# Retention and gated MLP on one core: the first chunk in 128-token blocks, weight flushing by a mask from ScalarE, and a new plan

## The chip, the core and the metric

The kernel runs on one core of one Trainium2 chip. The metric is the device time of one execution in microseconds; before the change it is 221.97 us, the median of three runs (221.79 to 222.39). All inputs start in HBM and the output ends there.

## What is computed

A retention layer (8 heads, 4 sequences of 768 tokens, head size 64) is followed by a gated MLP on the 512 joined columns:

```python
for t in range(S):
    state = gamma[None, :, None, None] * state + np.einsum('bhd,bhe->bhde', k[:, :, t], v[:, :, t])
    y[:, :, t] = scale * np.einsum('bhd,bhde->bhe', q[:, :, t], state)
x = y.transpose(0, 2, 1, 3).reshape(B, S, H * D)
for k in range(K):                       # K = 5, causal taps
    gate_pre += conv_w[k][None, None, :] * xp[:, k:k + S, :]
gate = 1.0 / (1.0 + np.exp(-gate_pre))
val = x @ w_val
return gate * val @ w_out
```

The weights come as 8-byte words and are turned into float32 on the chip; values below a threshold become zero.

## The kernel before, in words

The 768 tokens are cut into 6 chunks of 128, so there are 24 attention blocks (4 sequences per chunk), numbered chunk by chunk. Block `g` has one tile `att` of 1 MB (q and k by head column, v and k by token). POOL scales v by a decay (`decay`, L253). A block is worked as two 64-token halves in 64x64 pieces of the array: `scores` (L262), the triangle `mask` (L271, VectorE), `y_scores` and `y_state` (both recorded at L299), and `state` (L283), which adds to the running state `z_ps` in PSUM. `y_state` reads a copy of that state, `snap` (L294, ScalarE), one per half; in the first chunk the first half has none. `evac` (L344, VectorE) multiplies the result in PSUM by a decay table and writes it to the chunk's `x`. Function `block` issues on TensorE, in this order, `y_scores(g)`, the second `state` of `g`, the first `state` of `g+1`, `y_state(g)`, and `scores(g+1)`.

When the four blocks of a chunk are done, `x` of 512 tokens is ready. ScalarE rounds it to `xh` (L353), POOL makes the remainder `xl` (L357). `val` (L468) is 12 matmuls of 128x512 for each of 4 column groups: wvh by xh, wvl by xh, wvh by xl. The gate is a convolution of 5 taps: tap 0 on ScalarE (L443), the others on VectorE (L445), of which the planner may move taps 1 and 2 to TensorE (`pe_tap`, L454, by a diagonal matrix). Then come the sigmoid (L461), `gated` (L477), a split into gvh (L484) and gvl (L488), and `outp` (L496), 12 matmuls for each of 4 sequences. So 48 tiles of 12 matmuls follow one another over the program.

`convert` makes one of 8 weight tiles (and the small `cw`) in seven steps: VectorE `cv_bits` (L388), `cv_top` (L394), `cv_exp` (L400), `cv_rest` (L404), ScalarE `cv_size` (L409), POOL `cv_sum` (L413), VectorE `cv_flush` (L417). Then ScalarE rounds (L428) and POOL takes the remainder (`cv_low`, L432). Its working tile `acc` comes from a ring of two PSUM banks, which the convolution uses too.

The order on every engine is fixed when the program is built. Each step is entered with a due time, an engine, a cost and what it reads and writes (`at`); `plan` (L57) is a list scheduler that runs these costs forward and writes the steps out in the order in which it started them. Each engine then works through its own queue in that order, and an instruction that waits holds all that stand behind it. SP's queue issues the loads and stores, ScalarE's queue the four small loads. The constants that steer it are `EARLY`, `EARLY_AT`, `LATE_AT`, `MLP_AT`, `W_AT` and the like (from L532).

Of the kernel before, what the change touches and what calls it, by code (L numbers as in the profile page):

```python
# [16 lines left out]
P = 128  # L17
# [39 lines left out]
def plan(steps):  # L57
# [46 lines left out]
    for s in steps:  # L104
        clock.setdefault(s.engine, 0.0)
        if not s.waits:
            offer(s)
    order, words, paged, small = [], PAGE - 32, [0.0, 0.0], False
    while any(free.values()):
# [15 lines left out]
        clock[e] = start + s.cost  # L125
        if e == "PE" and s.words:

            left, now = s.words, start
            while left >= words:
                now += s.cost * words / s.words  # L130
# [5 lines left out]
            clock[e] = max(clock[e], now + s.cost * left / s.words)  # L136
# [17 lines left out]
def tile_retention_gated_mlp(  # L154
# [52 lines left out]

    small_sb = const.tile([P, small.shape[1]], F32, name="small_sb")
    vd_sb = small_sb[:, 0:48].rearrange("p (c x) -> p c x", x=8)
    ra_sb = small_sb[:, 48:72].rearrange("p (c x) -> p c x", x=4)  # L210
    tri_sb = small_sb[:, 72:136]
    pos_sb = const.tile([2, P + 512], F32, name="pos_sb")
# [20 lines left out]

    tiles, us, snaps, xs, xh, xl, decs, pos_ps = {}, {}, {}, {}, {}, {}, {0: base}, []
# [43 lines left out]
    def state(g, s):  # L278
        b, c = chunks[g]
        v, k = halves(g, 2), halves(g, 3)  # L280
        for j in range(2):
            for x, rows, cols in ((0, LO, LO), (1, LO, HI), (0, HI, HI), (1, HI, LO)):
# [4 lines left out]
                    start=g == 0 and s == 0 and j == 0, stop=True,  # L287
                    skip_group_check=True,
                )

    def snap(g, s):
        b, c = chunks[g]
        sn = mlp.tile([P, 2, 2, HALF], F32, name="snap", bufs=4)
        nc.scalar.copy(sn, z_ps[:, :, b])  # L294
        snaps[g, s] = sn

# [15 lines left out]
    def y_state(g):  # L312
        b, c = chunks[g]
        q = halves(g, 0)
        for s in (1, 0):
            if c == 0 and s == 0:
                continue
# [61 lines left out]
    def cv_bits(n):  # L379
        hi, _ = words(n)  # L380
        size = hi.shape[1]
        bits = ps_a.tile([P, 512], I32, name="acc")[:, 0:size]
        cvt[n] = (
            bits,
# [3 lines left out]
        nc.vector.tensor_scalar(  # L388
            bits, hi, 3, 0x3FFFFFFF, op0=ALU.logical_shift_left, op1=ALU.bitwise_and
# [8 lines left out]
    def cv_exp(n):  # L398
        bits, top, _ = cvt[n]
        nc.vector.tensor_scalar(bits, top, -0x800000, None, op0=ALU.bitwise_and)  # L400

    def cv_rest(n):
        bits, _, rest = cvt[n]
# [4 lines left out]
    def cv_size(n):  # L408
        nc.scalar.activation(cvt[n][0].bitcast(F32), words(n)[0].bitcast(F32), AF.Abs)  # L409

    def cv_sum(n):
        _, top, rest = cvt[n]
        nc.gpsimd.tensor_tensor(rest, rest, top.bitcast(F32), op=ALU.add)  # L413

    def cv_flush(n):
        bits, _, rest = cvt[n]
        nc.vector.scalar_tensor_tensor(  # L417
            cw_sb.rearrange("p a k -> p (a k)") if n == "cw" else rest,
            bits.bitcast(F32), TINY, rest, op0=ALU.is_ge, op1=ALU.mult,
# [112 lines left out]

    MM = 0.232
    EARLY = 6
    EARLY_AT = 8.0
    EARLY_STEP = 4.0
    LATE_AT = 29.71
    LATE_STEP = 6.095
    MLP_AT = 30.972
    MLP_STEP = 3.476  # L540
    SPLIT_LEAD = 5.44
    CONV_LEAD = 6.919
    W_AT = (9.3, 13.0, 15.63, 22.7, 36.8, 30.28, 34.86, 38.1)
# [3 lines left out]
    def load_at(due, g):  # L547
        loaded[g] = due
        a = [("att", g % LB, "qk"), ("att", g % LB, "vk")]
        if g == 0:  # L550
# [7 lines left out]
            for s in steps[-4:]:  # L558
                s.lag = 5.0
# [24 lines left out]

    def attention(g, t, before):
# [19 lines left out]
        pairs = 64 + 16 * (c < NCH - 1) + 48 * (g + 1 < NG) - 16 * (c == 0)  # L605
# [3 lines left out]
        if b == 0:  # L609
            xbufs[c] = Slot("x", XB)  # L610
            last = [xbufs[c - 1]] + [("x", c - 1, i) for i in range(B)] if c else []
# [213 lines left out]
```

## Time and profile before

| | |
|---|---|
| median of three runs | 221.97 us |
| the profiled execution's own time | 222.85 us |
| its span in the profile | 221.1 us |
| TensorE (PE) busy | 203.8 us, 92% |
| VectorE (DVE) busy | 136.4 us, 62% |
| ScalarE (ACT) busy | 104.6 us, 47% |
| GpSimd (POOL) busy | 105.6 us, 48% |
| moved by DMA | 36.32 MB |

The profile is of one execution. "Busy" is the time in which an engine had an instruction in work; times are from the span's start. The chain of waits follows the last instruction back to what released it, step by step, so its pieces add up to the span.

### The profile page before, as it was taken

The numbers are of one execution on the slowest core, as the hardware profiler recorded it, in microseconds if no ns is written. First come the engines' busy times: TensorE is split into PE (matmuls) and PEld (weight loads), VectorE is DVE, ScalarE is ACT, GpSimd is POOL, SyncE is SP. The second block draws the span as 40 slices with busy tenths as digits, with TensorE's granted clock in tenths as the row PEclk, the third lists the DMA queues.
The fourth block names the chain that finished last, engine by engine and source line by source line (L and its number), as shares of the span: only waits on it lengthen the run. The fifth ranks groups of instructions, "written<-read, shape, count | busy, mean of one in ns | idle before, by whom it ended". The sixth has DMA issues, their size and how long they took to land.

```text
span 221.1 us, 7950 instructions
## 1 busy us (share of the span) xinstructions
PE 203.8 (92%) x3553; PEld 162.8 (74%) x3553; DVE 136.4 (62%) x211; ACT 104.6 (47%) x218; POOL 105.6 (48%) x93
## 2 busy tenths in 40 slices
PE   8467369999799999999999999999999999999994
PEld 3266358887577888788887888788878888888883
DVE  0486577999998999478386376873397543911000
ACT  2472257562965566463383464534535336331311
POOL 0274868686999726644460934600924226220400
PEclk9857557999999999999999999999999999999999
DMA  6999998653364643564456444011011111111122
GB/s 196 417 421 417 409 396 341 256 193 101 138 203 184 238 129 160 193 204 159 136 224 235 167 119 205 1 52 47 7 50 47 47 47 50 47 47 47 47 98 95
DMA packets 8822, 36.32 MB, mean 164 GB/s; under 512 B 1106, under 2 KB 1618, under 8 KB 5844
## 3 DMA queue, kind: packets, MB, share of 16 engines
q1 hardware_dynamic: 8352, 35.66, 42.5%
q8 instruction: 28, 0.46, 0.9%
q10 hardware_dynamic: 436, 0.16, 0.3%
q14 instruction: 6, 0.05, 0.1%
HBM read 29.52 MB, written 6.29 MB: 162 GB/s over the span
## 4 chain that ended last, share of the span: by engine, by line
PE 82%; DVE 6%; DMA 5%; issue 3%; POOL 3%; SPq 0%; ACT 0%; POOLq 0%; ACTq 0%
PE mm L496 30%; PE mm L468 29%; PE sy L299 12%; PE z_ps L283 5%; PE sy L262 5%; DMA att<-in_att_dram 5%; DVE u L271 2%; POOL att L253 1%; DVE top L394 1%; DVE x L344 1%; PE acc L454 1%; POOL rest L413 1%; DVE acc L388 1%; POOL wol L432 1%; DVE gate L477 1%
## 5 line engine op out<-in xcount | busy, mean ns | idle before, releaser
L445 DVE SCALAR_TENSOR_TENSOR acc<-x,cw_sb,acc 128x512 f32<-128x512 f32 x93 | 67.9, 751 | 13.9 <-ACT acc L443 12.7
L357 POOL TENSOR_TENSOR xl<-x,xh 128x512 fp32r<-128x512 f32 x24 | 30.4, 1288 | 34.9 <-PE mm L468 22.4
L488 POOL TENSOR_TENSOR gvl<-gate,gvh 128x512 fp32r<-128x512 f32 x24 | 30.7, 1289 | 29.3 <-ACT gvh L484 19.6
L496 PE MATMUL mm<-wol,gvh 128*128 128x512 f32 (+1 forms) x100 | 39.2, 392 | 0.1
L253 POOL TENSOR_TENSOR att<-att,small_sb 128x512 f32<-128x512 f32 x24 | 25.0, 1043 | 29.9 <-DMA att<-in_att_dram 24.4
L496 PE MATMUL mm<-woh,gvh 128*128 128x512 f32 (+1 forms) x100 | 39.2, 392 | 0.0
L496 PE MATMUL mm<-woh,gvl 128*128 128x512 f32 (+1 forms) x100 | 38.6, 386 | 0.0
L468 PE MATMUL mm<-xh,wvh 128*128 128x512 f32 x96 | 28.1, 406 | 1.0 <-DVE gate L477 1.0
L477 DVE TENSOR_TENSOR gate<-mm,gate 128x512 f32<-128x512 f32 x24 | 16.5, 687 | 19.4 <-PE mm L468 18.9
L299 PEld LDWEIGHTS sy<-u,att 64*64 64x64 f32 x768 | 14.9, 148 | 17.8 <-DVE u L271 11.6
L506 ACT COPY o_sb<-mm 128x512 f32<-128x512 f32 (+1 forms) x25 | 14.3, 573 | 28.5 <-PE mm L496 28.4
L468 PE MATMUL mm<-xl,wvh 128*128 128x512 f32 x96 | 27.2, 399 | 0.1
L484 ACT CAST gvh<-gate 128x512 fp32r<-128x512 f32 x24 | 14.9, 621 | 26.0 <-DVE gate L477 18.7
L299 PE MATMUL sy<-u,att 64*64 64x64 f32 x768 | 18.4, 240 | 9.3 <-DVE u L271 9.3
L468 PE MATMUL mm<-xh,wvl 128*128 128x512 f32 x96 | 26.5, 396 | 0.0
L344 DVE TENSOR_TENSOR x<-sy,dec 128x512 f32<-128x512 f32 x20 | 13.7, 686 | 19.9 <-PE sy L262 19.7
L461 ACT ACTIVATE gate<-acc 128x512 f32<-128x512 f32 x24 | 14.3, 597 | 18.4 <-POOL gvl L488 13.2
L496 PEld LDWEIGHTS mm<-wol,gvh 128*128 128x128 f32 x100 | 18.8, 188 | 4.8 <-POOL wol L432 0.9
L468 PEld LDWEIGHTS mm<-xh,wvh 128*128 128x128 f32 x96 | 17.6, 188 | 5.9 <-ACT xh L353 1.8
L496 PEld LDWEIGHTS mm<-woh,gvh 128*128 128x128 f32 x100 | 18.8, 188 | 4.3
L496 PEld LDWEIGHTS mm<-woh,gvl 128*128 128x128 f32 x100 | 18.8, 188 | 4.0
L468 PEld LDWEIGHTS mm<-xl,wvh 128*128 128x128 f32 x96 | 17.8, 187 | 4.7 <-POOL xl L357 0.4
(46 smaller groups left out, 264.9 us busy)
## 6 DMA issues: line engine op xcount, KB each, us to landing
att<-in_att_dram SPq DMA_DIRECT2D x23, 1024.0 KB, 5.8
out_dram<-o_sb SPq DMA_DIRECT2D x23, 256.0 KB, 2.0
wst<-in_w_dram SPq DMA_DIRECT2D x8, 512.0 KB, 8.7
att<-in_att_dram SPq DMA_DIRECT2D x2, 512.0 KB, 5.1
out_dram<-o_sb SPq DMA_DIRECT2D x2, 128.0 KB, 1.7
small_sb<-in_small_dram ACTq DMA_DIRECT2D x1, 68.0 KB, 4.8
eye_sb<-in_eye_dram ACTq DMA_DIRECT2D x1, 64.0 KB, 8.9
cw_raw<-in_conv_w_dram ACTq DMA_DIRECT2D x1, 20.0 KB, 6.6
```

Source lines behind the costliest of these rows:

```text
L253: nc.gpsimd.tensor_tensor(v, v, vd_sb[:, c, :].unsqueeze(2).broadcast_to([P, 8, HALF]), op=ALU.mult)
L299: return nc.tensor.matmul(sy[cols, h, off:off + HALF], lhsT=lhsT, rhs=rhs, start=start, stop=True, skip_group_check=True,)
L344: nc.vector.tensor_tensor(xs[c][:, :, b, HALO:].rearrange("p (h j) t -> p h j t", h=2), sy[:, :, 256:512].rearrange("p h (j t) -> p h j t" ...
L357: nc.gpsimd.tensor_tensor(xl[n, ct], xs[n][:, ct, :, HALO:], xh[n, ct].bitcast(F32), op=ALU.subtract)
L445: nc.vector.scalar_tensor_tensor(acc, x[:, :, k:k + P], cw_sb[:, m, k:k + 1], acc, op0=ALU.mult, op1=ALU.add,)
L461: nc.scalar.activation(gate[n, m], accs.pop((n, m)), AF.Sigmoid)
L468: nc.tensor.matmul(vps[n, m], lhsT=w[:, m, ct * P:(ct + 1) * P], rhs=xx[n, ct].rearrange("p b t -> p (b t)"), start=(i == 0), stop=(i == 3 ...
L477: nc.vector.tensor_tensor(gv, vps.pop((n, m)), gv, op=ALU.mult)
L484: nc.scalar.copy(gvs[n, m][0], gate[n, m])
L488: nc.gpsimd.tensor_tensor(gvl, gate.pop((n, m)), gvh.bitcast(F32), op=ALU.subtract)
L496: nc.tensor.matmul(ops[n, b, cs.start][:, 0:cs.stop - cs.start], lhsT=gg[:, b * P:(b + 1) * P], rhs=w[:, ct, cs], start=(i == 0), stop=(i ...
L506: nc.scalar.copy(o_sb[:, 0:step], ops.pop((n, b, cs.start))[:, 0:step])
```

## The change

1. The four blocks of chunk 0 (no earlier state) are no longer cut into halves. `wide_scores` makes the 128x128 scores of each head with 64 contraction rows (two row halves of the array); two `wide_mask` steps on VectorE apply a 128x128 triangle; `wide_y` multiplies by v over all 128 tokens, with the result in a bank of the `mm` ring in the layout of `x`; `wide_state` adds all 128 tokens to the state. There is no `snap` in these blocks. `wide_evac` reads the `mm` bank. The host lays v, k and the decay of chunk 0 out by whole tokens, and `small` grows by the triangle, from 136 to 264 columns.
2. `convert`: ScalarE makes a mask in three passes (`cv_size`, `cv_sign`, `cv_keep`) ahead of `cv_bits`, which now ands with it; `cv_exp` writes to SBUF in place of PSUM; `cv_sum` writes the result, and `cv_flush` is gone.
3. The planner knows a slow TensorE clock, the start constants are new, the first weight tile is loaded ahead of the first attention tile, and ScalarE's table load stands ahead of the four small loads.

```diff
+    def wide_scores(g):
+        q, kT = tiles[g][:, 0], tiles[g][:, 1]
+        for x in range(2):
+            for j in range(2):
+                for r, rows in enumerate((LO, HI)):
+                    nc.tensor.matmul(
+                        sy[:, r, (2 * x + j) * P:(2 * x + j + 1) * P],
+                        lhsT=kT[rows, x, j, :], rhs=q[rows, x, j, :],
+                        start=True, stop=True, skip_group_check=True,
+                    )
+    def wide_mask(g, r):
+        us[g, r] = mlp.tile([P, UT], F32R, name="gvl", bufs=GV)...
+        nc.vector.tensor_tensor(us[g, r], sy[:, r]..., wide_sb..., op=ALU.mult)
+    def wide_y(g):
+        ys[g] = ps_m.tile([P, NPAIR, P], F32, name="mm")
+        for ct in range(NPAIR):
+            for i, cols in enumerate((LO, HI)):
+                x, r, j = place(2 * ct + i)
+                nc.tensor.matmul(
+                    ys[g][cols, ct], lhsT=v[:, 2 * ct + i], rhs=u[r][:, 2 * x + j],
+                    start=True, stop=True, skip_group_check=True,
+                )
+    def wide_state(g):
...
+                nc.tensor.matmul(
+                    z_ps[(LO, HI)[r], x, b, j], lhsT=k[:, 2 * ct + i], rhs=v[:, 2 * ct + i],
+                    start=g == 0 and j == 0, stop=True, skip_group_check=True,
+                )
+    def wide_evac(g):
+        nc.vector.tensor_tensor(xs[0][:, :, g, HALO:], ys.pop(g), base, op=ALU.mult)
...
+        nc.scalar.activation(cvt[n][0].bitcast(F32), hi.bitcast(F32), AF.Abs)
+    def cv_sign(n):
+        nc.scalar.activation(m, m, AF.Sign, bias=tiny[:, 0:1])
+    def cv_keep(n):
+        nc.scalar.activation(m, m, AF.Relu, scale=KEEP)
     def cv_bits(n):
-        nc.vector.tensor_scalar(
-            bits, hi, 3, 0x3FFFFFFF, op0=ALU.logical_shift_left, op1=ALU.bitwise_and
+        nc.vector.scalar_tensor_tensor(
+            bits, words(n)[0], 3, bits, op0=ALU.logical_shift_left, op1=ALU.bitwise_and
         )
     def cv_exp(n):
-        nc.vector.tensor_scalar(bits, top, -0x800000, None, op0=ALU.bitwise_and)
+        nc.vector.tensor_scalar(rest.bitcast(I32), top, -0x800000, None, op0=ALU.bitwise_and)
     def cv_rest(n):
-            rest, words(n)[1], 2.0 ** -36, bits.bitcast(F32), op0=ALU.mult, op1=ALU.mult
+            rest, words(n)[1], 2.0 ** -36, rest, op0=ALU.mult, op1=ALU.mult
-    def cv_flush(n):
-            bits.bitcast(F32), TINY, rest, op0=ALU.is_ge, op1=ALU.mult,
...
-    EARLY = 6
-    EARLY_AT = 8.0
-    EARLY_STEP = 4.0
-    LATE_AT = 29.71
-    W_AT = (9.3, 13.0, 15.63, 22.7, 36.8, 30.28, 34.86, 38.1)
+    FIRST_LOADS = ((1, 0), (0, 0), (0, 1), (0, 2), (1, 1), (0, 3), (1, 2), (1, 3), (0, 4))
+    EARLY = 8
+    WIDE_AT = 5.173
+    WIDE_STEP = 2.417
+    LATE_AT = 15.786
+    W_AT = (7.61, 15.38, 16.24, 22.7, 36.8, 30.28, 34.04, 43.78)
```

What the plan makes of it, at three places. TensorE, the blocks of chunk 0: before, one such block (`sy` the scores and the result, `u` the masked scores, `z_ps` the state):

```order
L299 MATMUL sy<-u,att 64x64 x16
L283 MATMUL z_ps<-att 64x64 x16
L299 MATMUL sy<-att,snap 64x64 x8
L262 MATMUL sy<-att 64x64 x16
L299 MATMUL sy<-u,att 64x64 x16
```

TensorE at the same place now, from the last two blocks of chunk 0 (L328 scores, L353 result, L364 state) over block 4 to the first matmuls of the MLP (L549):

```order
L328 MATMUL sy<-att 128x128 x8
L353 MATMUL mm<-gvl,att 64x128 x8
L364 MATMUL z_ps<-att 64x64 x8
L305 MATMUL z_ps<-att 64x64 x8
L284 MATMUL sy<-att 64x64 x16
L535 MATMUL acc<-x,diag 128x512
L378 MATMUL sy<-u,att 64x64 x16
L305 MATMUL z_ps<-att 64x64 x16
L378 MATMUL sy<-att,snap 64x64 x16
L284 MATMUL sy<-att 64x64 x16
L549 MATMUL mm<-xh,wvh 128x512 x4
```

The next block's scores stand behind this block's state, as before behind `y_state`; block 4 still stands ahead of the first MLP matmul, and a tap by the diagonal matrix (L535) has come in front of block 4.

ScalarE around the end of chunk 0, before (L409 `cv_size`, L428 the rounded weight, L294 `snap`, L443 tap 0, L353 the rounded `x`):

```order
L428 CAST wvh<-rest 128x512
L294 COPY snap<-z_ps 128x256
L409 ACTIVATE acc<-wst 128x512
L294 COPY snap<-z_ps 128x256
L443 ACTIVATE acc<-x,cw_sb 128x512
L339 COPY x<-x 128x16x4
L332 ACTIVATE dec<-base,small_sb 128x128
L353 CAST xh<-x 128x512 x3
L428 CAST wvh<-rest 128x512
```

ScalarE there now (L464, L468, L472 the three mask passes, L509 the rounded weight, L430 the rounded `x`):

```order
L464 ACTIVATE acc<-wst 128x512
L468 ACTIVATE acc<-acc,tiny 128x512
L315 COPY snap<-z_ps 128x256
L472 ACTIVATE acc<-acc 128x512
L416 COPY x<-x 128x16x4
L524 ACTIVATE acc<-x,cw_sb 128x512
L315 COPY snap<-z_ps 128x256 x2
L509 CAST wvh<-rest 128x512
L430 CAST xh<-x 128x512 x4
L524 ACTIVATE acc<-x,cw_sb 128x512
```

The casts of `x` now stand behind two snapshots of the state in block 4 and a weight, where before they stood behind tap 0.

POOL from the third weight on, now (L275 decay, L498 `cv_sum`, L513 the weight's remainder, L434 the remainder of `x`); before, two `xl` stood ahead of the fourth `wvl`, and the other two a decay behind it:

```order
L498 TENSOR_TENSOR rest<-rest,top 128x512
L275 TENSOR_TENSOR att<-att,small_sb 128x512
L513 TENSOR_TENSOR wvl<-rest,wvh 128x512
L434 TENSOR_TENSOR xl<-x,xh 128x512
L498 TENSOR_TENSOR rest<-rest,top 128x512
L275 TENSOR_TENSOR att<-att,small_sb 128x512
L513 TENSOR_TENSOR wvl<-rest,wvh 128x512
L434 TENSOR_TENSOR xl<-x,xh 128x512 x3
```

Between the first and the second `xl` there are now three other steps. TensorE has 2 taps by the diagonal matrix in place of 3, VectorE 94 in place of 93.

## Rows read from the trace of the kernel before

**Rows 1.** The page: busy time by engine, clock in 40 slices, one load.

```profile
PE 203.8 (92%) x3553; PEld 162.8 (74%) x3553; DVE 136.4 (62%) x211; ACT 104.6 (47%) x218; POOL 105.6 (48%) x93
...
PEclk9857557999999999999999999999999999999999
...
small_sb<-in_small_dram ACTq DMA_DIRECT2D x1, 68.0 KB, 4.8
```

**Rows 2.** Chain of waits, chunk 0 to first MLP matmuls: start, length, what.

```profile
1.17 5.64 DMA att<-in_att_dram
...
16.05 1.14 PE sy L299 x32
...
18.89 0.75 PE sy L262 x31
...
21.01 0.69 PE sy L299 x32
...
22.18 1.91 issue
...
31.60 0.69 DVE x L344
...
32.94 1.13 PE sy L299 x32
34.07 0.85 PE z_ps L283 x32
...
36.57 1.59 PE mm L468 x6
38.15 0.86 PE acc L454 x2
```

**Rows 3.** Chain of waits, later: a tile and a block at the full clock.

```profile
80.63 2.52 PE mm L468 x10
83.16 2.80 PE mm L496 x12
85.96 0.62 PE sy L299 x32
86.58 0.47 PE z_ps L283 x32
```

**Rows 4.** Windows: busy time of each engine, then the granted clock.

```profile
36.50:66.00 29.50, 27.61 (x711) 21.36 (x705) 28.70 (x47) 18.10 (x41) 24.12 (x22) 1.00 0.52 185
66.00:72.50 6.50, 6.44 (x144) 4.76 (x145) 5.59 (x10) 3.83 (x9) 6.50 (x6) 1.00 0.48 171
```

**Rows 5.** Windows of half a microsecond in which the granted clock changed.

```profile
19.00:19.50 0.50, 0.50 (x28) 0.46 (x23) 0.00 (x0) 0.00 (x0) 0.46 (x1) 0.70 0.97 401
22.50:23.00 0.50, 0.00 (x0) 0.00 (x0) 0.47 (x2) 0.00 (x0) 0.50 (x1) 0.71 0.94 393
36.00:36.50 0.50, 0.50 (x25) 0.43 (x20) 0.00 (x0) 0.50 (x3) 0.50 (x1) 0.64 0.76 287
```

**Rows 6.** Timeline, POOL and ScalarE: start, length, engine, line, what.

```profile
10.91 1.04 POOL L253 TENSOR_TENSOR att<-att,small_sb 128x512 f32<-128x512 f32 x1 [2.91 <-DMA att<-in_att_dram]
19.04 1.04 POOL L253 TENSOR_TENSOR att<-att,small_sb 128x512 f32<-128x512 f32 x1 [0.30 <-DMA att<-in_att_dram]
33.39 1.64 ACT L353 CAST xh<-x 128x512 fp32r<-128x512 f32 x3
34.07 2.52 POOL L357 TENSOR_TENSOR xl<-x,xh 128x512 fp32r<-128x512 f32 x2 [1.32 <-ACT xh L353]
```

**Rows 7.** Groups on VectorE up to 72 us: busy us, mean ns.

```profile
L400 DVE TENSOR_SCALAR acc<-top 128x512 int32<-128x512 int32 x8 | 5.5, 687 | 0.1
L417 DVE SCALAR_TENSOR_TENSOR rest<-acc,rest 128x512 f32<-128x512 f32 x8 | 5.5, 684 | 0.2 <-POOL rest L413 0.2
```

**Rows 8.** The same view on ScalarE up to 72 us.

```profile
L294 ACT COPY snap<-z_ps 128x256 f32<-128x256 f32 x20 | 6.8, 373 | 3.7 <-PE z_ps L283 3.5
L409 ACT ACTIVATE acc<-wst 128x512 f32<-128x512 f32 x8 | 5.2, 646 | 3.4 <-DVE rest L404 3.3
```

More of the change, by code (lines that the diff above doesn't have):

```diff
@@ L104, in plan @@
     for s in steps:
-        clock.setdefault(s.engine, 0.0)
+        clock.setdefault(s.engine, 2.2 if s.engine == "DMA" else 0.0)
         if not s.waits:
@@ L108, in plan, with dim, light @@
     order, words, paged, small = [], PAGE - 32, [0.0, 0.0], False
+    lit = {}
+    def dim(t):
+        w = int((t - FIRST) // GRID)
+        return w > 0 and lit.get(w - 1, 0.0) < 0.7 * GRID
+    def light(a, b):
+        while a < b:
+            w = int((a - FIRST) // GRID)
+            end = min(b, FIRST + (w + 1) * GRID)
+            lit[w] = lit.get(w, 0.0) + end - a
+            a = end + 1e-9
     while any(free.values()):
@@ L124, in plan @@
             small = s.small
-        clock[e] = start + s.cost
+        cost = s.cost * (DIM if e == "PE" and s.words and dim(start) else 1.0)
+        clock[e] = start + cost
         if e == "PE" and s.words:
@@ L135, in plan @@
             words -= left
-            clock[e] = max(clock[e], now + s.cost * left / s.words)
+            clock[e] = max(clock[e], now + cost * left / s.words)
+        if e == "PE":
+            light(start, clock[e])
         for t in s.next:
@@ L286, in state @@
                     rhs=v[rows, x, j, s, :],
-                    start=g == 0 and s == 0 and j == 0, stop=True,
-                    skip_group_check=True,
+                    start=False, stop=True, skip_group_check=True,
                 )
@@ L377, in words, with cv_size @@
         return raw[:, :, 1], lo16
-    def cv_bits(n):
+    def cv_size(n):
         hi, _ = words(n)
         size = hi.shape[1]
-        bits = ps_a.tile([P, 512], I32, name="acc")[:, 0:size]
         cvt[n] = (
-            bits,
+            ps_a.tile([P, 512], I32, name="acc")[:, 0:size],
             stage.tile([P, size], I32, name="top"),
@@ L563, in first_block @@
     def first_block():
-        scores(0)
-        state(0, 0)
+        state(B, 0)
+        scores(B)
     def block(g):
@@ L583, in tile_retention_gated_mlp, with first_attention @@
     scored, whole = {}, {}
+    def first_attention(g, t):
+        qk, vk = ("att", g % LB, "qk"), ("att", g % LB, "vk")
+        sc, u, y = Slot("s", 1), [Slot("gvl", GV), Slot("gvl", GV)], Slot("mm", 2)
+        at(t, "POOL", 1.0, ["small"], [vk], decay, g)
+        at(t, "PE", WIDE * 0.85, [qk], [sc], wide_scores, g)
+        steps[-1].words, steps[-1].small = 16, True
+        for r in range(2):
+            at(t + 0.1, "DVE", 0.6, [sc, "small"], [u[r]], wide_mask, g, r)
+        at(t + 0.2, "PE", WIDE * 1.5, [vk] + u, [y, "z"], wide_out, g)
+        steps[-1].words, steps[-1].small = 32, True
+        if g == 0:
+            xbufs[0] = Slot("x", XB)
+            at(0.0, "DVE", 0.14, [], [xbufs[0]] + [("x", 0, i) for i in range(B)], new_x, 0)
+        whole[0] = t + 4.1
+        at(t + 0.3, "DVE", 0.6, [y, "base", xbufs[0]], [("x", 0, g)], wide_evac, g)
+        load_at(t + 0.4, g + LB)
+        at(t + 1.45, "ACT", 0.3, ["base", "small"], [("dec", 1)], table, 1, g)
     def attention(g, t, before):
@@ L610, in attention @@
             xbufs[c] = Slot("x", XB)
-            last = [xbufs[c - 1]] + [("x", c - 1, i) for i in range(B)] if c else []
-            at(t + 0.5, "ACT" if c else "DVE", 0.14, last,
-               [xbufs[c]] + [("x", c, i) for i in range(B)], new_x, c)
+            last = [xbufs[c - 1]] + [("x", c - 1, i) for i in range(B)]
+            at(t + 0.5, "ACT", 0.14, last, [xbufs[c]] + [("x", c, i) for i in range(B)], new_x, c)
         whole[c] = t + 3.1
```

122 lines of the change are left out of this document (80 added, 42 removed).

## The prediction

> **What bounds the kernel now.** I read the page first. TensorE is busy for 92% of the span, and its clock row is full from slice 8 on [rows 1]; only the first 36 us, where the clock row shows mostly 5 to 8 tenths, leave it much slack. The chain of waits says what holds it there. Chunk 0's four blocks run one behind the other (TensorE, VectorE, TensorE again), the `evac` of the last one is at 31.60, block 4 follows, and the first MLP matmul comes at 36.57 [rows 2]. From there to 72.5 us TensorE is busy for 27.61 of 29.50 and 6.44 of 6.50 us, so it stands idle for 1.95 us [rows 4]; after that it never waits for long. From the first MLP matmul on the work is the same in both kernels, except for the taps: 48 tiles at 2.80 [rows 3], which is 134.4 us, and 19 attention blocks. So the time moves by three things alone: when that first matmul starts, the taps that TensorE loses, and what it stands idle after it.
>
> In that stretch VectorE is the fullest of the others, 28.70 of 29.50 us, POOL has 24.12 and ScalarE 18.10 [rows 4].
>
> **The price of a wide block.** No such instruction is in the trace. The nearest one with the whole array is the tap: two float32 passes of 512 columns in 0.86 us [rows 2], so 0.107 us for 128 columns at the full clock. Scores are 8 matmuls of two passes, 16 passes: 1.72 us if none overlap, 0.86 if the two row halves do. The old 64x64 pieces overlap four deep: 32 passes in 0.47 us [rows 3] are 0.015 us each, where 64 columns alone would take 0.054. I take the overlap: scores 0.86, result 0.86, state 0.43 at the full clock, twice that at half. Two masks of about 0.65 (an `evac` of that size took 0.69, [rows 2]) take 1.3. Going from 64x64 pieces to the whole array costs 0.19: ten matmuls after a block took 2.52, where ten twelfths of 2.80 are 2.33 [rows 3]; I take 0.2 once per block, between state and the next scores, since the switch ahead of the result falls into the wait for the masks. With 0.1 for hand-overs a block repeats every 3.75 us at the full clock and 5.9 at half.
>
> The Trainium skill (TensorEngine Tiling (Array Packing), Key Properties) says that a change of tiling mode drains the array, and its Theoretical Speedup puts 64x64 pieces at four tiles: that speaks against this change, which goes from four pieces to two and switches modes inside a block. The 0.19 us agrees that a switch costs something; were both switches of a block paid in full, it would add 0.2 in each of four blocks, 0.8 us.
>
> **Which clock.** The clock rose at 19.0 to 19.5, after TensorE had worked from 16.05 without a break to 19.6, and at 36.0 to 36.5, after it had worked since 32.94; it fell at 22.5 to 23.0, after a stretch with waits [rows 2, 5]. In the wide blocks TensorE works 4.5 of 5.9 us at half clock, but 2.3 of 3.75 at full. I expect it to rise and fall again, and take the middle.
>
> **When x of chunk 0 is ready.** The first tile's two halves landed at 1.17 + 5.64 = 6.8 [rows 2]. Now a 0.5 MB weight goes first, so the half that the scores need lands then and the other about 1.3 us later (0.5 MB at some 410 GB/s, the DMA's rate at 401 in [rows 5]). The small loads go out 1.3 us later behind the table load; with 4.8 us to land [rows 1] the triangle is there by about 7, ahead of the first mask. Scores 7.0 to 7.9, masks behind the first weight's `cv_bits` to 9.2, result and state at half clock to 11.9; the second tile has the same bytes ahead of it as before and landed at 10.9 [rows 6]. So the second scores start at 12.1. Two more turns (2 x 3.75 to 2 x 5.9) bring the fourth scores to 19.6 to 23.9; its tile, with 0.5 MB less ahead of it than when it landed at 19.04 [rows 6], is there at 17.8 and does not hold it. Scores, masks, result and `evac` add 3.9 to 5.6: x is ready at 23.5 to 29.5. I take 26.5, against 32.3 before. The fetch stall of 1.91 us [rows 2] lies in the old blocks, which have 112 matmuls where a wide one has 24; I count it as gone with them.
>
> **The first MLP matmul.** By the order, it no longer waits only for x. From 26.5: the halo copy and tap 0 on ScalarE 0.9 to 27.4; the new tap on TensorE 0.86 to 1.7, say 1.3, to 28.7; the result of block 4 and its state, 1.13 + 0.85 = 2.0 at half clock [rows 2], to 30.7; the snapshot 0.37 [rows 8], a weight's cast 0.52 and the first cast of x 0.62 to 32.2. I take 32.3 (27.9 with the full clock throughout, 35.6 with half), against 36.57: **4.3 us earlier**.
>
> **Taps.** Three taps of 0.86 lay behind that point; one is left there, one lies ahead of it, one goes to VectorE: **1.7 us less**. VectorE's extra tap is covered by what it loses: in each weight one 0.684 instruction goes [rows 7], 8 of them, against four more masks and that tap, 5.5 less 3.4 us. `cv_exp` (0.687 with PSUM as its target, [rows 7]) I leave at that. The Trainium skill (VectorE: DVE Perf Modes, The perf-mode tier table) gives a float32 `tensor_scalar` from SBUF to SBUF twice the rate; the row, with PSUM as its target, neither shows nor denies it. By it each would take about half, some 2 us less on VectorE in all (an estimate).
>
> **What TensorE waits for afterwards.** (a) The first four matmuls are paced by casts of x, 0.51 each (three in 1.64 start to end, [rows 6]) where a matmul takes 0.23: 0.9 more than now. (b) Block 5 stands behind seven matmuls, to 34.9, but its mask stands on VectorE behind a tap that needs ScalarE's next tap 0, which is behind the four casts: 33.6 + 0.63, then tap, `evac` and mask, 36.2: 1.3. (c) The second `xl` is on POOL behind `wvl`, `xl`, a sum, a decay and `wvl`: from 31.6, five of 1.25 and one of 1.04, to 38.8, and the third 1.25 later: 0.7. (d) Block 6's mask stands behind `cv_bits` of the fifth weight, which waits for three ScalarE passes: 0.7. After this I halve what there is now (1.95), for VectorE has more room: 1.0. Together 4.6 against 1.95: **2.7 us back**.
>
> **The sum.** 4.3 + 1.7 - 2.7 = 3.3 us. The span goes from 221.1 to 217.8. The profiled execution took 222.85, 0.88 above the median; against the median the prediction is 221.97 - 3.3 = **218.7 us**.
>
> **Rivals.**
> *Full clock in the wide blocks* (0.23). For it: they leave shorter gaps than the old ones. The first MLP matmul comes at 27.9, but POOL and the loads have not moved with it: I give 1.5 more waiting. 8.7 + 1.7 - 4.2 = 6.2, 215.8 us; without the 1.5, 214.3.
> *Half clock all through* (0.13). For it: at half clock the new turn of 5.9 is no shorter than an old one, 16.05 to 21.01 [rows 2]. First matmul at 35.6, waits 2.2 above now: 1.0 + 1.7 - 2.2 = 0.5, 221.5 us, no change; up to 1.2 more waiting gives 222.7.
> *ScalarE sets the pace, slower* (0.14). Between 36 and 72 four weights bring 8 further ScalarE passes of about 0.6 (0.646 each, [rows 8]), 4.8 us, on an in-order queue that also holds snapshots, casts and sigmoids. VectorE's `cv_bits` waits for the third pass with `evac` and masks behind it. Against it: ScalarE had 11 us free there [rows 4]. It decides once each such wait reaches TensorE in full: 3.3 - 4.8 = -1.5, 223.5 us.
> The forecast keeps 0.50.
>
> **Range and chances.** 214.3 (the full clock without further waits) to 222.7 (half clock with them) leaves out most of the ScalarE case and a little below, under 2 in 10. What a measurement can tell from no change is about 0.3%, 0.67 us: 221.3 to 222.6. Faster: 0.47 of the forecast, 0.23, and 0.04 of the half-clock case, 0.74. Same 0.10, mostly the half-clock case. Slower 0.16.
>
> **What would show it.** Right: a first MLP matmul near 32, x of chunk 0 ready near 26 with a clock that changes in between, the `xh` casts coming only after block 4's snapshots, and some 4 to 5 us of TensorE idle between there and 70. Wrong: scores of 128 columns above 1 us at full clock; a first matmul before 29 or after 35; VectorE's `cv_bits` waiting over a microsecond for ScalarE again and again.

## The result, and the profile after

The changed kernel took 220.57 us (median of 17 runs, 219.48 to 222.55), the kernel before 222.21 us beside it (17 runs, 221.44 to 224.27): a ratio of 0.9916, with a 95% interval of 0.9889 to 0.9944. It is faster, by 1.64 us where 3.3 were forecast. The two profiled executions lie further apart, 219.93 against 222.85 us, and their spans by 3.0, since the one of before is above its median and the one of after below. Twelve of the 17 executions of the changed kernel took 219.48 to 221.34 us and five 221.86 to 222.55; the profiled one is among the twelve.

The page of after, busy time and clock, which answers to [rows 1]:

```profile
PE 202.7 (93%) x3295; PEld 160.3 (74%) x3295; DVE 137.8 (63%) x207; ACT 112.0 (51%) x232; POOL 108.1 (50%) x94
...
PEclk9889999999999999999999999999999999999999
```

The clock row has gone to full almost everywhere; the busy times have hardly moved. Windows of after, as in [rows 4, 5]: stretch, length, then busy time of PE, PEld, DVE, ACT and POOL, the granted clock, the DMA share and GB/s.

```profile
9.00:10.00 1.00, 0.63 (x9) 0.63 (x10) 0.97 (x3) 0.96 (x4) 0.31 (x1) 0.80 1.05 432
10.00:13.00 3.00, 3.00 (x38) 2.88 (x36) 2.89 (x6) 2.34 (x10) 2.10 (x2) 0.50 0.99 411
13.00:14.00 1.00, 0.60 (x10) 0.41 (x8) 0.76 (x3) 0.77 (x2) 0.67 (x3) 0.99 1.10 455
14.00:20.00 6.00, 4.42 (x69) 3.74 (x70) 3.84 (x7) 5.46 (x14) 3.03 (x3) 1.00 1.02 415
20.00:26.00 6.00, 3.40 (x64) 2.93 (x59) 5.83 (x10) 2.23 (x4) 3.64 (x3) 1.00 1.01 421
...
32.35:72.50 40.15, 35.88 (x860) 27.52 (x857) 37.93 (x59) 27.57 (x58) 37.43 (x31) 1.00 0.57 213
```

In this stretch the clock is at its lower level (0.50) from within the window of 9 to 10 us (0.80) to 13 us only. From the first MLP matmul to 72.5 us TensorE stands idle for 40.15 - 35.88 = 4.27 us, and VectorE (37.93) and POOL (37.43) are both over 93% busy there.

TensorE's timeline around the end of chunk 0 (start, length, what, and in brackets how long it had waited and for what; `issue` is a wait for nothing that the profile names, and the last section ties it to the fetch of instructions):

```profile
16.48 1.16 PE L328 MATMUL sy<-att 64*128 64x128 f32 x16
18.52 1.48 PE L353 MATMUL mm<-gvl,att 128*64 128x128 f32 x15 [0.89 <-DVE gvl L336]
...
20.51 1.16 PE L328 MATMUL sy<-att 64*128 64x128 f32 x16
24.17 1.49 PE L353 MATMUL mm<-gvl,att 128*64 128x128 f32 x15 [2.50 <-DVE gvl L336]
...
28.16 1.13 PE L535 MATMUL acc<-x,diag 128*128 128x512 f32 x2 [0.48 <-ACT acc L524]
...
31.62 0.28 PE L378 MATMUL sy<-att,snap 64*64 64x64 f32 x3 [0.79 <-issue]
...
32.35 1.20 PE L549 MATMUL mm<-xh,wvh 128*128 128x512 f32 x4
...
35.11 0.69 PE L378 MATMUL sy<-u,att 64*64 64x64 f32 x32 [0.87 <-DVE u L293]
...
37.95 0.39 PE L378 MATMUL sy<-att,snap 64*64 64x64 f32 x11 [1.35 <-issue]
```

VectorE at the same place, which shows why the fourth block's result waited 2.5 us, where the third's had waited 0.89 (the fourth's scores were done at 21.67):

```profile
20.48 0.43 DVE L488 TENSOR_SCALAR rest<-top 128x512 int32<-128x512 int32 x1
20.94 0.69 DVE L492 SCALAR_TENSOR_TENSOR rest<-wst,rest 128x512 f32<-128x512 uint16 x1
21.55 0.69 DVE L476 SCALAR_TENSOR_TENSOR acc<-wst,acc 128x512 int32<-128x512 int32 x1
22.14 0.69 DVE L374 TENSOR_TENSOR x<-mm,base 128x512 f32<-128x512 f32 x1
22.74 0.68 DVE L482 SCALAR_TENSOR_TENSOR top<-wst,acc 128x512 int32<-128x512 int32 x1
23.34 1.28 DVE L336 TENSOR_TENSOR gvl<-sy,small_sb 128x512 f32<-128x512 f32 x2
24.54 0.42 DVE L488 TENSOR_SCALAR rest<-top 128x512 int32<-128x512 int32 x1
24.99 1.65 DVE L492 SCALAR_TENSOR_TENSOR rest<-wst,rest 128x512 f32<-128x512 uint16 x1
26.56 0.68 DVE L374 TENSOR_TENSOR x<-mm,base 128x512 f32<-128x512 f32 x1
```

The fourth block's masks (L336) stand behind the conversions of two weights, and its `wide_evac` behind a `cv_rest` (L492) of 1.65 us. The last `wide_evac` (L374) ends at 27.24; before, x of chunk 0 was ready at 32.29 [rows 2].

### The profile page after: what moved, and what is told of

Read it like the earlier page. It is cut to its first block, busy times and chain, and to the rows that moved or that the text cites. A ratio compares the mean times of both kernels' runs of the same rounds, so it can differ in the third digit from the quotient of the medians.

```text
span 218.1 us, 7442 instructions
## 1 busy us (share of the span) xinstructions
PE 202.7 (93%) x3295; PEld 160.3 (74%) x3295; DVE 137.8 (63%) x207; ACT 112.0 (51%) x232; POOL 108.1 (50%) x94
## 4 chain that ended last, share of the span: by engine, by line
PE 74%; DVE 10%; DMA 6%; issue 3%; ACT 3%; POOL 2%; SPq 0%; DVEq 0%; POOLq 0%; ACTq 0%
PE mm L577 31%; PE mm L549 26%; PE sy L378 8%; DMA att<-in_att_dram 6%; PE sy L284 3%; PE z_ps L305 3%; DVE acc L526 2%; DVE rest L492 1%; PE mm L353 1%; DVE gvl L336 1%; PE sy L328 1%; DVE top L482 1%; DVE acc L476 1%; DVE rest L488 1%; POOL att L275 1%
## 5 line engine op out<-in xcount | busy, mean ns | idle before, releaser
L526 DVE SCALAR_TENSOR_TENSOR acc<-x,cw_sb,acc 128x512 f32<-128x512 f32 x94 | 68.7, 751 | 13.8 <-ACT acc L524 12.6
L434 POOL TENSOR_TENSOR xl<-x,xh 128x512 fp32r<-128x512 f32 x24 | 31.2, 1316 | 33.1 <-PE mm L549 22.8
L569 POOL TENSOR_TENSOR gvl<-gate,gvh 128x512 fp32r<-128x512 f32 x24 | 31.3, 1314 | 30.8 <-ACT gvh L565 21.0
L275 POOL TENSOR_TENSOR att<-att,small_sb 128x512 f32<-128x512 f32 x24 | 25.9, 1082 | 26.7 <-DMA att<-in_att_dram 23.2
L549 PE MATMUL mm<-xh,wvh 128*128 128x512 f32 x96 | 28.0, 405 | 1.4 <-DVE gate L558 0.8
L549 PE MATMUL mm<-xh,wvl 128*128 128x512 f32 x96 | 27.4, 398 | 0.0
L549 PE MATMUL mm<-xl,wvh 128*128 128x512 f32 x96 | 27.3, 398 | 0.0
L549 PEld LDWEIGHTS mm<-xh,wvh 128*128 128x128 f32 x96 | 17.4, 188 | 6.6 <-DVE gate L558 1.6
L549 PEld LDWEIGHTS mm<-xl,wvh 128*128 128x128 f32 x96 | 17.9, 188 | 4.4
L549 PEld LDWEIGHTS mm<-xh,wvl 128*128 128x128 f32 x96 | 17.9, 188 | 4.3
L315 ACT COPY snap<-z_ps 128x256 f32<-128x256 f32 x40 | 13.7, 373 | 11.1 <-PE z_ps L305 9.5
```

What stands on the lines that cost most here:

```text
L275: nc.gpsimd.tensor_tensor(v, v, vd_sb[:, c, :].unsqueeze(2).broadcast_to([P, 8, HALF]), op=ALU.mult)
L434: nc.gpsimd.tensor_tensor(xl[n, ct], xs[n][:, ct, :, HALO:], xh[n, ct].bitcast(F32), op=ALU.subtract)
L526: nc.vector.scalar_tensor_tensor(acc, x[:, :, k:k + P], cw_sb[:, m, k:k + 1], acc, op0=ALU.mult, op1=ALU.add,)
L549: nc.tensor.matmul(vps[n, m], lhsT=w[:, m, ct * P:(ct + 1) * P], rhs=xx[n, ct].rearrange("p b t -> p (b t)"), start=(i == 0), stop=(i == 3 ...
L569: nc.gpsimd.tensor_tensor(gvl, gate.pop((n, m)), gvh.bitcast(F32), op=ALU.subtract)
```

## The experiments

The theory after the result: the blocks of whole tokens bring x of chunk 0 forward, and part of that is given back because VectorE and POOL are full afterwards. (TensorE's own waits bear out little of the second half. From the first MLP matmul to 72.5 us it waited 2.0 us for VectorE, 1.8 before; the 2.3 us more of idle time are mostly 1.35 for instructions, 0.59 for ScalarE and 0.23 for POOL.) The rivals: the clock alone did it; the cheaper conversion did it; the new plan did it, whatever the parts.

In the table "start" is the first MLP matmul and "idle" TensorE's idle time from there to 72.5 us, both of the profiled execution (in e4 and e8 one or two matmuls of the MLP stand ahead of block 4, in the others four or more behind it); the ratio is against the kernel before.

| run | start | idle | clock there | span | ratio, 95% interval |
|---|---|---|---|---|---|
| before | 36.50 | 1.95 | 1.00 | 221.1 | |
| after | 32.35 | 4.27 | 1.00 | 218.1 | 0.9916, 0.9889 to 0.9944 |
| after, run again | 34.06 | 2.49 | 0.97 | 218.8 | 0.9896, 0.9861 to 0.9931 |
| e1, exponent in PSUM | 35.71 | 1.84 | 0.97 | 219.4 | 0.9919, 0.9881 to 0.9958 |
| e2, masks first | 33.16 | 2.76 | 1.00 | 218.1 | 0.9898, 0.9861 to 0.9936 |
| e3, before with filler | 36.42 | 4.08 | 0.95 | 223.1 | 1.0101, 1.0067 to 1.0134 |
| e4, blocks alone | 31.20 | 4.81 | 0.87 | 224.2 | 1.0126, 1.0079 to 1.0173 |
| e5, conversion alone | 35.85 | 3.17 | 0.91 | 228.9 | 1.0280, 1.0239 to 1.0322 |
| e6, a tap on VectorE | 36.41 | 2.10 | 0.97 | 220.6 | 0.9946, 0.9910 to 0.9981 |
| e7, weights later | 33.57 | 2.92 | 1.00 | 218.1 | 0.9947, 0.9914 to 0.9980 |
| e8, blocks, new constants | 32.02 | 2.21 | 0.97 | 219.8 | 0.9921, 0.9886 to 0.9956 |
| e9, conversion, new constants | 36.78 | 3.89 | 0.90 | 224.3 | 1.0182, 1.0143 to 1.0220 |
| e10, planner alone | 34.86 | 2.28 | 1.00 | 218.2 | 0.9938, 0.9907 to 0.9968 |
| e11, after, new constants | 34.72 | 1.12 | 0.96 | 219.9 | 0.9981, 0.9944 to 1.0018 |

**The changed kernel again** (no edit).

> The changed kernel unchanged, as the reference for the runs beside it. Both theories expect what was measured: 0.5 to 1.1% below the kernel before, first MLP matmul at 32 to 33 us in the profile, granted clock about 0.99.

220.25 us (8 runs). Its profile differs from that of after mainly in blocks 4 and 5 (same views as above):

```profile
32.96 0.28 PE L378 MATMUL sy<-att,snap 64*64 64x64 f32 x3 [2.12 <-issue]
...
34.06 2.07 PE L549 MATMUL mm<-xh,wvh 128*128 128x512 f32 x4
```

```profile
34.06:72.50 38.44, 35.95 (x855) 27.70 (x853) 36.21 (x55) 26.28 (x56) 34.93 (x30) 0.97 0.55 197
```

The same program waited 2.12 us for its instructions in block 4 there, where the other execution waited 0.79 in block 4 and 1.35 in block 5. So it began the MLP 1.71 us later and then stood idle for 2.49 in place of 4.27 us, 1.35 of the difference being a wait that merely lay on the other side of the first matmul. Its clock was at the lower level from 34.06 to 36.5 us (four matmuls took 2.07 us in place of 1.20), and its span is 0.7 longer. So start and idle time of the table must be read together, and this pair does not tell what an earlier start is worth.

**The exponent back in PSUM.** In after, `cv_exp` and `cv_rest` have very different lengths (groups on VectorE to 72 us: busy us, mean ns, idle before):

```profile
L492 DVE SCALAR_TENSOR_TENSOR rest<-wst,rest 128x512 f32<-128x512 uint16 x8 | 8.1, 1009 | 0.1
L476 DVE SCALAR_TENSOR_TENSOR acc<-wst,acc 128x512 int32<-128x512 int32 x8 | 5.5, 690 | 5.6 <-ACT acc L472 5.6
...
L488 DVE TENSOR_SCALAR rest<-top 128x512 int32<-128x512 int32 x8 | 5.0, 623 | 0.4
L488 DVE TENSOR_SCALAR rest<-top 128x20 int32<-128x20 int32 x1 | 1.2, 1219 | 0.0
```

```diff
-        nc.vector.tensor_scalar(rest.bitcast(I32), top, -0x800000, None, op0=ALU.bitwise_and)
+        nc.vector.tensor_scalar(bits, top, -0x800000, None, op0=ALU.bitwise_and)
-            rest, words(n)[1], 2.0 ** -36, rest, op0=ALU.mult, op1=ALU.mult
+            rest, words(n)[1], 2.0 ** -36, bits.bitcast(F32), op0=ALU.mult, op1=ALU.mult
```

> The changed kernel in exactly the same order on every engine; only cv_exp writes its result to PSUM again and cv_rest reads it there, so that cv_exp no longer runs from SBUF to SBUF and cv_rest no longer reads two tensors in SBUF. Theory (VectorE and POOL get in each other's way in these two steps, and this gives back part of the gain): cv_exp takes a flat 0.69 us, cv_rest a flat 0.68 instead of 0.68 to 1.65, POOL's decay falls from 1.10 to 1.04 us and its remainders from 1.37 to 1.28, TensorE stands idle 1 to 2 us less after the first MLP matmul, and the time is 0.5 to 2 us lower than the changed kernel's. Rival (those waits are covered): the durations change the same way, but the time stays within 0.5 us; if the longer hold of the acc bank costs, it is up to 1 us higher.

Both are even again, and their sum per weight falls from 1.63 to 1.38 us:

```profile
L488 DVE TENSOR_SCALAR acc<-top 128x512 int32<-128x512 int32 x8 | 5.5, 692 | 0.2
L492 DVE SCALAR_TENSOR_TENSOR rest<-wst,acc 128x512 f32<-128x512 uint16 x8 | 5.5, 683 | 0.4
```

The time did not follow: 220.44 us, no different from after. That the loss of 0.25 us a weight lies beside other work is not shown by it, since the `acc` bank is now held longer: VectorE waited 0.86 us for ScalarE's pass into it at 21.86, the fourth result 3.73 us for its masks (2.50 in after), and with 2.39 us for instructions in block 4 the MLP began at 35.71.

**The masks ahead of the third weight.**

```diff
+    last = [s for s in steps if s.fn is wide_mask and s.args[0] == B - 1]
+    for s in steps:
+        if s.fn is cv_bits and s.args[0] == 2:
+            s.after = last
```

> The changed kernel with one more rule for the planner: the third weight's cv_bits comes after the masks of the last block of chunk 0. Theory (x of chunk 0 is late because those masks stand behind the conversion on VectorE): x ready at about 25.5 instead of 27.2 us, first MLP matmul 1 to 1.5 us earlier, time 0.5 to 1.5 us lower than the changed kernel's. Rival (after this point VectorE and POOL hold, not x): x is earlier, but the time stays within 0.5 us or rises, since the third and fourth weights come later.

The fourth result waited 1.30 us for its masks in place of 2.50, but x of chunk 0 came only 0.2 earlier (the last `evac` began at 26.35), since other waits took over: by the profile 2.0 us for a weight's rounding on ScalarE and 1.6 for an attention tile. 220.28 us, no different from after.

**The kernel before, kept busy.**

```diff
+        if g < 5:
+            junk = Slot("mm", 2)
+            for i in range(4):
+                at(t + 0.01, "PE", 0.2, [], [junk], fill, g, i)
```

> The kernel before with four idle matmuls of 128x512 in bf16 behind each of the first five blocks on TensorE, into a free bank of the mm ring, so that TensorE has fewer gaps there; they take no part in the result. Rival (the gain of the change is the clock alone): the granted clock of the first 36 us rises to 0.9 or more, the first MLP matmul moves from 36.6 to 33 us or earlier, and the time falls to 219 to 220.5 us. Theory (the shorter chain is most of it: three hand-overs less in each block): the clock rises, but the first MLP matmul moves by less than 2 us, and the time stays at 221 to 223 us.

```profile
20.00:31.00 11.00, 6.50 (x226) 4.71 (x228) 6.84 (x11) 3.68 (x8) 8.10 (x7) 0.84 1.01 411
```

From 20 to 31 us the granted clock was 0.84, against 0.62 in the kernel before, and over the first 36 us 0.91 against 0.67; but the last `evac` began at 31.32 (31.60 before) and the MLP at 36.42. What the faster blocks gained, the idle matmuls themselves (four took 1.04 us at the full clock) and longer waits for instructions (5.0 us up to 36.4, 2.6 before) took. 224.61 us. So a faster clock did not bring the gain by itself here. That does not rule the clock out as a part of it, since the idle matmuls stand in TensorE's queue and the planner also made 1 tap on TensorE out of 3.

**One part at a time, with the constants as they stood.** e4 is the changed kernel with the old `convert`; e5 is the kernel before with the new one (parts 1 and 2 of the diff shown ahead), each with the constants of the kernel it was made from.

> The changed kernel with the old weight conversion (VectorE's fourth instruction per weight back, no mask passes on ScalarE), the order worked out anew by the same planner. Theory (the gain is the earlier x of chunk 0, which the whole-token blocks alone bring; VectorE's and ScalarE's shares lie beside TensorE): 220 to 221 us, within 0.7 of the changed kernel, x of chunk 0 ready at 26 to 28. Rival (the blocks' masks need the room that the cheaper conversion gives on VectorE): x ready after 28.5, 221.5 us or more.

> The kernel before with the new weight conversion alone, 64-token blocks as before, planned anew with the constants of before. Theory: x of chunk 0 no earlier than 31, since the old blocks set it, first MLP matmul at about 36.5, no change within 0.7 us (221.5 to 222.9 us). Rival (VectorE, busy for 28.7 of 29.5 us after that matmul, held the kernel before): 1 to 2 us faster. Rival from the forecast (ScalarE's two extra passes a weight set the pace): slower by 1 us or more.

Both were far slower, 225.97 and 228.73 us, which neither theory had; the open-ended rivals had such numbers (over 221.5 us with x after 28.5; slower by 1 us or more). In e4 x was ready at 28.78 and the MLP began at 31.20, earlier than in any other run, though with only two of its matmuls ahead of block 4 (the third came at 36.88), and more than the gain was lost later:

```profile
44.85 0.74 PE L378 MATMUL sy<-u,att 64*64 64x64 f32 x32 [2.07 <-DVE u L293]
...
65.11 0.49 PE L545 MATMUL mm<-xl,wvh 128*128 128x512 f32 x1 [1.98 <-POOL xl L434]
```

```profile
31.20:72.50 41.30, 36.49 (x841) 28.70 (x841) 37.66 (x61) 23.74 (x51) 33.88 (x29) 0.87 0.57 201
```

Two waits of 2 us, and the mean clock of the stretch fell to 0.87, so that the matmuls behind each wait took longer too. In e5 the planner gave TensorE 7 taps where it had 3, four of 0.86 us [rows 2], 3.4 us, and TensorE is busy for 208.1 us in place of 203.8. So these two runs mix the part with a plan that was not made for it; e8 to e11 do the same again with constants of their own.

**The tap ahead of block 4, on VectorE.**

```diff
+        early = next(s for s in planned if s.fn is pe_tap and s.args[:2] == (0, 0))
+        early.fn = tap
+        planned.remove(early)
+        planned.insert(nxt, early)
```

> The changed kernel, with the convolution tap that TensorE does ahead of block 4 given to VectorE, ahead of its own first tap; nothing else moved. Theory (the way to the first MLP matmul leads over that tap, and TensorE loses its 0.86 us): first MLP matmul up to 0.7 earlier and 0.5 to 0.9 us less in all. Rival (what TensorE waits for next, VectorE's masks of block 5 behind the taps, moves back by the 0.73 of the tap there): the wait for the mask of block 5 grows by about 0.7, no change within 0.4 us.

222.25 us, the interval overlapping that of after: the 0.5 to 0.9 us that the theory expected did not come. Nor did the rival's longer wait for the mask of block 5, for which TensorE did not wait at all. Its profiled execution is a poor test of the single step, since chunk 0 itself was 1.35 us later there (28.59, where the profile names a tile that landed late and POOL's decay); block 4 then waited for its mask, and for instructions:

```profile
30.70 0.69 PE L378 MATMUL sy<-u,att 64*64 64x64 f32 x32 [0.84 <-DVE u L293]
...
35.15 0.37 PE L378 MATMUL sy<-att,snap 64*64 64x64 f32 x2 [2.84 <-issue]
```

**Weights of the second half loaded later.**

```diff
-    LOAD_W_AT = (16.88, 13.65, 14.03, 26.79)
+    LOAD_W_AT = (26.0, 20.0, 23.0, 30.0)
```

> The changed kernel, with one second-half weight load queued behind one, and another behind two, more attention loads; the order on all engines but the DMA queue's is the same. Theory (instruction fetches wait for the crowded DMA, which moves some 410 GB/s up to 35 us): the fetch stalls of TensorE, 2 us in two places around the first MLP matmul, shrink only if the DMA is less crowded by 36 us; the loads moved are 1 MB of 14, so 0 to 0.5 us less. Rival (the attention tiles come earlier, GpSimd's wait of 1.6 us for one at 43.7 goes): the wait goes and the time stays, as GpSimd's sum there is not waited for.

The rival's account: POOL's wait for a tile at 43.7 is gone, it waits for VectorE in its place, and the interval overlaps that of after (221.99 us; the profiled span is that of after, 218.1, with the MLP 1.2 us later and 1.35 us less idle time).

```profile
43.75 1.29 POOL L498 TENSOR_TENSOR rest<-rest,top 128x512 f32<-128x512 f32 x1 [0.63 <-DVE rest L492]
```

**Each part with a plan of its own.** The start constants were searched anew for each, with the changed kernel's planner and its own model. e8: blocks, old `convert`. e9: old blocks, new `convert`. e10: old blocks, old `convert`, so that only the planner and its constants differ from before. e11: all of the change, searched on.

```diff
...
-        clock[e] = start + s.cost
+        cost = s.cost * (DIM if e == "PE" and s.words and dim(start) else 1.0)
+        clock[e] = start + cost
...
-    LATE_AT = 29.71
-    W_AT = (9.3, 13.0, 15.63, 22.7, 36.8, 30.28, 34.86, 38.1)
+    LATE_AT = 28.91
+    W_AT = (6.44, 12.14, 18.17, 28.19, 34.46, 28.94, 29.71, 34.56)
```

(The core of e10's, shortened; its planner also counts more for an instruction fetch while loads run and a later first load. The others have the same planner and constants of their own.)

> As the run with the blocks and the old conversion, but with the start constants searched anew for it with the planner's own model. In that run x of chunk 0 was early (evac ended at 28.8, first MLP matmul 31.2) and 3 to 5 us were lost later, to masks, to a late xl and to two spells of half clock. Theory (that was a plan made for other work; the blocks bring the gain): the loss after 40 us goes, 219.5 to 221.5 us. Rival (VectorE, ScalarE and GpSimd cannot keep up after an early start as long as VectorE has a fourth instruction per weight): waits for masks or xl over 2 us remain, 222.5 us or more.

> The kernel before with the new conversion alone, with the changed kernel's planner and start constants searched anew with its model. Theory (chunk 0's old blocks set the first MLP matmul, so relief on VectorE is worth little): first MLP matmul 35.5 to 37, 221.5 to 223 us, no change. Rival (what the conversion costs elsewhere, two SBUF instructions on VectorE that slow down beside GpSimd and three passes of ScalarE ahead of cv_bits, stays): 224 us or more, with waits on POOL's or VectorE's chain after 60 us as in the run before.

> The kernel before with blocks and conversion as they were, but the changed kernel's planner (it knows a slow clock) and start constants searched anew with its model. Theory (the gain is the parts', not the plan's): 221.5 to 224 us, no change or slower. Rival (the gain is the new plan's): 220.8 us or less.

> The changed kernel with its start constants searched on in the same way and for as long; nothing else. It tells how far two plans for the same work lie apart, and so what the three runs beside it can mean. Theory (a plan of the same work that looks as good to the planner is as good within 1 us): 219.5 to 221.5 us. Rival (the plan decides as much as the parts, since each wait that it does not foresee costs 1 to 2 us): over 222 us.

e10 is the surprise: 221.46 us, with an interval wholly below the kernel before, and a profiled span of 218.2, with neither the blocks nor the conversion. VectorE, TensorE and the windows of e10:

```profile
29.41 0.69 DVE L361 TENSOR_TENSOR x<-sy,base 128x512 f32<-128x512 f32 x1 [3.24 <-PE sy L279]
```

```profile
34.13 0.27 PE L316 MATMUL sy<-att,snap 64*64 64x64 f32 x2 [1.76 <-issue]
...
34.86 1.20 PE L485 MATMUL mm<-xh,wvh 128*128 128x512 f32 x4
```

```profile
34.86:72.50 37.64, 35.36 (x978) 28.22 (x977) 36.80 (x60) 22.14 (x49) 33.59 (x30) 1.00 0.67 227
```

x is ready at 30.10 in place of 32.29, the first matmul comes 1.64 us earlier although instructions were waited for, TensorE has 2 taps in place of 3, and idles for 2.28 us. With the taps, 1.64 + 0.86 - 0.33 = 2.2 of the 2.9 us by which its span is shorter.

Its clock from 20 to 31 us was 0.69 (0.62 before, 1.00 in after), so it reached the span of after without the full clock in chunk 0.

e8, the blocks with a fitting plan, is as fast as after (221.12 us), so e4's loss was its plan. e11, the whole change in another plan, is not measurably faster than the kernel before (222.66 us): its rival, that the plan decides as much as the parts, had this. e9 stays slower, 226.82 us, in the rival's range, and shows how one wait costs twice (timelines of TensorE and VectorE, then windows):

```profile
47.66 1.13 PE L318 MATMUL sy<-u,att 64*64 64x64 f32 x32 [3.12 <-DVE x L363]
```

```profile
46.93 0.68 DVE L363 TENSOR_TENSOR x<-sy,dec 128x512 f32<-128x512 f32 x1
```

```profile
44.00:48.00 4.00, 0.88 (x15) 0.46 (x17) 3.90 (x7) 3.66 (x8) 2.75 (x3) 0.81 0.44 182
48.00:52.00 4.00, 4.00 (x130) 3.79 (x123) 4.00 (x7) 2.06 (x5) 3.32 (x3) 0.50 0.15 25
```

From 38.97 on VectorE had not stood idle for over 0.2 us: `cv_exp` took 1.28 and `cv_rest` 1.65 us there beside POOL, then came three taps, `cv_bits` and `cv_top`; behind them all stood the mask of the next block, a further `cv_exp` and the `evac` (L363) that the matmul waited for. TensorE waited 3.1 us, and the clock was then at its lower level (0.50) for the next 4 us.

## Why the prediction was right, and where it was not

**First matmul, taps, idle time: near the forecast, in part by luck.** x of chunk 0 at 27.24 (forecast 26.5), first MLP matmul at 32.35 (32.3), one tap fewer on TensorE, 4.27 us idle to 72.5 (4.6), span 218.1 (217.8). The sum held in this profile; from its rows the terms are 4.15 + 1.7 - 2.3 = 3.5, against 3.0 by which the span fell, so 0.5 us stays unplaced. The way to the first matmul was not the one forecast, which led over snapshot, weight and cast of x on ScalarE. Those were done in time:

```profile
29.33 2.17 ACT L430 CAST xh<-x 128x512 fp32r<-128x512 f32 x4
```

The matmul stood behind 0.79 us for instructions in block 4 and the scores of block 5, which the forecast did not have in that sum, and block 4 at the full clock made up for it. The medians moved by 1.64 us, half of what was forecast, with executions of the changed kernel spread over 3 us. Which term the medians take the other half from is not shown: the terms were measured in single executions, and in the same program "4.3 us earlier" and "2.7 us back" shift against each other when a wait for instructions falls on the other side of the first matmul.

**The clock: the condition of a rival came true, its result did not.** The forecast expected a clock that rises and falls; it was full from 13 us on. A block took 4.03 us (16.48 to 20.51), near the 3.75 forecast for the full clock. But the fourth result waited 2.50 us for masks behind weight conversions (0.89 is the ordinary wait, in the second and third block), and the last `wide_evac` stood behind a `cv_rest`: from the fourth scores to x it took 6.73 us, where the forecast had 3.9 to 5.6, and the rival had no term for that. So x came at the time of a half-clock mixture for another reason: that step of the forecast was right in its number and wrong in its cause.

**Price of a block.** Scores took 1.16 us from first start to last end, between the 0.86 of the forecast (row halves side by side) and the 1.72 of none overlapping; over 1 us was one of the forecast's signs of being wrong. The turn came out near all the same because two errors met. From scores to result it took 2.04 us (2.16 forecast), since the result began after the first of the two masks, and result, state and switch took 1.99 (1.59 forecast). What a switch costs alone no row shows. The draining at mode switches that the Trainium skill (TensorEngine Tiling (Array Packing), Key Properties) speaks of may be in these 0.4 us a block. (The four tiles for 64x64 pieces, which the forecast cites beside it, stand in The Solution on the same page of the Trainium skill.)

**Waits afterwards.** (a) did not show: the casts of chunk 0 came in time. (b) was 0.87 for 1.3. (c) and (d) did not reach TensorE. In their place came 1.35 us for instructions in block 5 (and 0.79 in block 4, ahead of the first matmul), a stall that the forecast counted as gone with the old blocks of chunk 0, and which came in the next ones; the rest is small waits up to 66 us, 0.77 for gates and 0.59 for a cast of the second chunk among them. The total agreed by compensation.

**ScalarE sets the pace.** Not in this plan: VectorE's `cv_bits` waited 5.6 us in all for the third mask pass, 5.56 of it for the first weight, ahead of all its other work, and no row of TensorE's waits names ScalarE but the 0.59 and 0.48 above. In e4 and e9, which were slower, the long waits of TensorE after the first MLP matmul were for VectorE and POOL.

**`cv_exp`.** Taken at 0.687; it was 0.43 with POOL idle and up to 1.0 us beside POOL, 0.623 on average. By the Trainium skill (VectorE: DVE Perf Modes, The perf-mode tier table) a float32 instruction of this kind would take about half, some 0.34 us (an estimate); the rows of this one, on int32, come near that (0.43) only while POOL is idle.

**What the prediction missed.** It gave the gain to the blocks. e10 has none of them and e8 has no new conversion, and the intervals of after, e8 and e10 overlap, while e11 with all of it gains nothing that can be measured. What is shown is that a new plan of the old work is enough for a gain of 0.6% (interval 0.3 to 0.9), where the whole change has 0.8% (0.6 to 1.1), and that two plans of the same work lie nearly as far apart as the change (ratios 0.9916 and 0.9981). What in the new plan does it is not shown: no run has the old planner with constants searched anew, so the planner's slow clock and the search are not told apart. The new conversion, which the forecast counted as relief for VectorE, made the old blocks slower in both plans tried (e5 by 2.8%, e9 by 1.8%), and the blocks are as fast without it (e8). What the blocks are worth on top of a fitting plan is below what these runs can tell. So the forecast's time lies in its range, but the cause of the gain that it named is not shown. Open is also why the wait for instructions at block 4 varies from 0.8 to 2.8 us between executions; the loads moved in e7 left 1.3 us of it.

No run beat the changed kernel beyond the intervals; e2 (0.9898) differs by nothing from the changed kernel run again beside it (0.9896).

## What to carry to other kernels

When a stage of the busiest engine starts earlier, add up by cause what that engine then waits for before giving the start its full worth: here 2.3 of 4.15 us came back as idle time, and the largest part, 1.35 us, was for instructions and not for the engines that looked full. A kernel whose order comes from a planner has to be compared with a new plan of the old work, or the gain may be put down to the wrong part: the forecast here gave to the blocks what a new plan without them nearly reached. And a part tested in a plan made for another cannot be told from that plan.

## What the runs showed of the hardware

**VectorE waits for POOL, instruction by instruction.** It does so in `cv_exp` and `cv_rest`, whose operands all lie in SBUF. In after, `cv_exp` took 0.43 us at 20.48, while POOL was idle. For a tile of 20 columns it took 1.22 us while POOL was adding, and ended 0.03 us after POOL did:

```profile
12.01 1.22 DVE L488 TENSOR_SCALAR rest<-top 128x20 int32<-128x20 int32 x1
```

```profile
11.94 1.26 POOL L498 TENSOR_TENSOR rest<-rest,top 128x512 f32<-128x512 f32 x1
```

The same instruction took 0.18 in the runs e2 and e7, where it began before POOL's addition; there the next one, `cv_rest`, took 1.15 and ended 0.03 to 0.04 us after POOL's. On 512 columns, whenever POOL had an instruction in work as VectorE's began, `cv_exp` ended 0.28 to 0.29 us and `cv_rest` 0.55 us after POOL's (five and four times up to 72 us in after). So the price depends on how much of POOL's instruction is left: nothing at 24.54 (0.42 us, POOL's ended at 24.67), but at 24.99 `cv_rest` took 1.65 us in place of the 0.69 of 20.94. POOL's instruction beside it, which ended at 26.09, took 1.46, where others of its line took 1.28:

```profile
24.63 1.46 POOL L513 TENSOR_TENSOR wvl<-rest,wvh 128x512 fp32r<-128x512 f32 x1
```

With one input in PSUM (e1) `cv_rest` stayed at 0.68. The Trainium skill (GPSIMD Engine Reference, Specifications) says that the two share their SBUF interfaces, with contention for VectorE instructions in a two-port mode or with two SBUF inputs; the rows agree, and give the price: up to 1 us for one instruction. POOL pays too: its decay took 1.104 us on average up to 72 us in after, 1.053 in e1 and 1.041 in the kernel before.

**TensorE's waits called `issue` follow the fetch of instructions.** The page of after lists a DMA queue that carries instructions alone, in packets of 16 KB:

```profile
q8 instruction: 26, 0.43, 0.8%
```

In the traces of all runs, 23 of TensorE's waits called `issue` in the first 100 us ended 1.26 to 1.62 us after such a packet had ended: in block 4 at 31.62 in after (packet to 30.26), 32.96 in the run again (31.54) and 35.15 in e6 (33.81). In the run again the packet began 1.15 us later than in after, at the same place of TensorE's work; why is open. The waits of about 0.5 us ahead of block 4's first `state` have no such packet near them.
